# Hourglass attention ahead of a gated FFN on one core: a new order of work in each slot, and small softmax columns moved into PSUM

## The chip, the cores and the metric

The kernel runs on one core of a Trainium2 chip. The metric is device time in microseconds, the median of several executions. The engines named below are the profile's: PE is TensorE (PEld its weight loads), DVE is VectorE, ACT is ScalarE, POOL is GpSimd, SP is SyncE; a "q" behind a name is the engine's instruction queue, which also issues transfers.

## The reference

Two stages in a row. Inputs are q, k and v of shape 8 x 8 x 576 x 64 (batch, heads, tokens, head size) and three FFN matrices, all float32. Cut to what matters:

```
q_d, k_d, v_d = means over 4 tokens in a row            # 576 -> 144 tokens
out_d  = softmax(q_d k_d^T / 8) v_d                     # pooled attention, 144 x 144
local  = softmax over the keys with |i - j| < 4 of (q k^T / 8), times v
x      = repeat(out_d, 4 tokens) + local                # rows (batch, token), 8 heads side by side: 4608 x 512
out    = (relu(x w_gate) * (x w_val)) w_out             # 512 -> 1536 -> 512
```

## The kernel before

**Tiling.** Two heads form a pair, so there are 32 pairs; four pairs fill the 512 columns of one batch of 576 rows of x. For a pair, q and k are loaded as float32 (`nat`), cast to float16 (`h16`, `cast_qk`: the half i=0 on ACT at L222, i=1 on POOL at L224), and turned so that the head size lies on partitions (`qkT`). v is loaded in windows of 32 tokens with a margin of 3 on both sides (`vst`) and cast on POOL (L230). Pairs below `NPE` = 12 are turned by PE matmuls against an identity (`turn_qk_pe`, `t_ps`), from which ACT (L265, two pieces) and DVE (L262, one) copy out of PSUM; pairs from 12 on are turned by DMA transposes that SP issues.

**Attention of a pair.** POOL adds four neighbours of `qkT` in two steps (`pool_qk`: `t`, L275, then `qkd`, L278). PE makes the local scores (36 matmuls into two banks, L288, `s_ps`), the pooled scores (4 matmuls into two banks, L302, `d_ps`), and the pooled v (12 matmuls, L312 and L321, `v_ps`, which ACT copies at L360 to `vd`). The local softmax on DVE adds the mask (L333), takes the row maximum `mx` (L352) and subtracts it (L353); ACT takes the exponential `e` (L381); DVE sums (L386), inverts (`rl`, L388) and multiplies (L393) to the weights `en`. The pooled softmax takes maxima on DVE (`max_d`: L341 twice, scaled to `nb` at L344), exponentials with a running sum on ACT (`exp_d`, L369, two instructions for each of the two heads), the reciprocal `rd` of the sums on DVE (L403) and a multiplication on POOL (`weights_d`, L410: two instructions) to `adn`. Both weights are turned (`turn_a_pe`: PE transposes into `a_ps`, L433 and L438, ACT copies L434 `at` and L439 `adt`; from pair 12 on by DMA). `outputs` then makes the local output (36 matmuls, L448, `u_ps`) and the pooled one (8 matmuls, L465, `o_ps`, which ACT copies to `od`), and DVE adds both into `xT` (L478).

**FFN.** A chunk has 512 rows. A task "h" is 8 matmuls of 512 columns for 128 of the 1536 hidden units (L494, two banks `h1_ps`, `h2_ps`), a Relu on ACT (L502) and a product on DVE (L504); a task "y" is 12 matmuls of 512 columns (L510), an ACT copy (L518) and a store of 128 rows. The list `ffn` holds, for each chunk, four times three h and a y of the chunk before; the first chunk has an empty entry in place of y.

**Order.** The kernel is recorded in a manual order: each engine runs its instructions in the order in which `slot(n)` issues them, and waits only through semaphores. `slot(n)` runs for n from -2 to 33. It handles pair n's scores and softmax, pair n-1's turned weights and outputs (pair n-2's from 12 on), pair n+1's turned q and k and its pooling, and pair n+2's casts (n+3's from 12 on). `quota` lets it take FFN entries: none for n below 4, three for n = 4 to 13, then four. `ffn_do` takes one entry, or none as long as its rows of x aren't made. What remains of the list after the slots runs alone. All PSUM results take turns in one pool of eight banks.

Of the kernel before, what the change touches and what calls it, by code (L numbers as in the profile page):

```python
# [17 lines left out]
VR = 112  # L18


def _np_constants():


    mask = np.full((96, 6, 38), NEG, np.float32)
    for blk in range(6):
        for p in range(96):
            w = 6 * (blk // 2) + 2 * (p // 32) + blk % 2
            t = 32 * w + p % 32
            for c in range(38):
                key = 32 * w - 3 + c  # L30
                if 0 <= key < 576 and abs(key - t) < 4:
                    mask[p, blk, c] = 0.0


    pool = np.zeros((VR, 9, 128), np.float16)
    for l in range(9):
        for par in range(2):
            for r in range(32):
                t = 16 * l + 8 * par + r // 4
                for col in [t] if l < 8 else [t - 128, 96 + t - 128]:  # L40
                    pool[64 * par + 3 + r, l, col] = 0.25
    return mask, pool, np.eye(96, dtype=np.float16)


# [5 lines left out]
def kernel(  # L50
# [57 lines left out]

    cons = pool("consts", 1)
    mask_sb = cons.tile([96, 6, 38], FP32, name="mask_sb")  # L110
    pool_sb = cons.tile([VR, 9, 128], FP16, name="pool_sb")
    eye_sb = cons.tile([96, 96], FP16, name="eye_sb")
    nc.scalar.dma_start(eye_sb, eye_dr)
    nc.scalar.dma_start(mask_sb, mask_dr)
    nc.scalar.dma_start(pool_sb, pool_dr)
    p_v16 = pool("v16", 7)
# [5 lines left out]
    p_ed = pool("ed", 2)  # L122
    p_vd = pool("vd", 4)
    p_od = pool("od", 2)
    psum = ctx.enter_context(tc.tile_pool(name="psum", bufs=8, space=bass.MemoryType.PSUM))

    for t in v_t:
        nc.gpsimd.memset(t[32:64], 0.0)
# [7 lines left out]
    def bank(shape, name, dt=FP32):  # L136
        return psum.tile(shape, dt, name=name, tag="bank")
# [68 lines left out]

    def cast_qk(p, i):
        s = st[p]
        if i == 0:
            s["h16"] = p_16.tile([96, 2, 768], FP16, name="h16", tag="h16")  # L210
        if p < NPE:
            src = s["nat"].rearrange("p a c -> p (a c)").rearrange(
                "p (b h f d) -> p h b f d", b=3, h=2, f=4
            )[:, i]
            dst = s["h16"].rearrange("p a c -> p (a c)").rearrange(
                "p (b f h d) -> p h b f d", b=3, h=2, f=4
            )[:, i]
        else:
            src = s["nat"][:, i].rearrange("p (h j d) -> p h j d", h=2, j=6)
            dst = s["h16"][:, i].rearrange("p (j h d) -> p h j d", h=2, j=6)  # L220
        if i == 0:
            nc.scalar.copy(out=dst, in_=src)  # L222
        else:
            nc.gpsimd.tensor_copy(out=dst, in_=src)  # L224
            s.pop("nat")

    def cast_v(p):
        s = st[p]
# [66 lines left out]

    def scores_d(p):
        s = st[p]
        qkd, v16 = s.pop("qkd"), s["v16"]
        s["dp"] = dp = [bank([80, 2, S // 4], "d_ps") for _ in range(2)]
        for c in range(2):  # L300
            for h in range(2):
                nc.tensor.matmul(  # L302
                    out=dp[h][:, c, :],
                    lhsT=qkd[64 * h : 64 * h + 64, 0, 64 * c : 64 * c + 80],
                    rhs=qkd[64 * h : 64 * h + 64, 1, :],
                    start=True,
                    stop=True,
                )
        s["vp"] = vp = bank([128, 4, D], "v_ps")
        v2 = v16.rearrange("p (h l) d -> p h l d", h=2)  # L310
        for l in range(8):
            nc.tensor.matmul(  # L312
                out=vp[:, 0:2, :],
                lhsT=pool_sb[:, l, :],
                rhs=v2[:, :, l, :],
                start=(l == 0),
                stop=(l == 7),
            )
        for c in range(2):
            for h in range(2):  # L320
                nc.tensor.matmul(  # L321
                    out=vp[64 * h : 64 * h + 64, 2 + c, :],
                    lhsT=pool_sb[:, 8, 64 * c : 64 * c + 64],
                    rhs=v2[:, h, 8, :],
                    start=True,
                    stop=True,
                )
# [9 lines left out]
    def max_d(p):  # L337
        s = st[p]
        s["nb"] = nb = p_st.tile([80, 4], FP32, name="nb", tag="nb")
        for h in range(2):  # L340
            nc.vector.tensor_reduce(  # L341
                out=nb[:, 2 * h : 2 * h + 2], in_=s["dp"][h], axis=AX.X, op=ALU.max
            )
        nc.vector.tensor_scalar(  # L344
            out=nb, in0=nb, scalar1=-SCALE / 16.0, scalar2=None, op0=ALU.mult
        )

    def shift_l(p):

        sm = st[p]["sm"]  # L350
        mx = p_st.tile([96, 12], FP32, name="mx", tag="mx")
        nc.vector.tensor_reduce(out=mx, in_=sm, axis=AX.X, op=ALU.max)  # L352
        nc.vector.tensor_tensor(  # L353
            out=sm, in0=sm, in1=mx[:, :, None].to_broadcast([96, 12, 38]), op=ALU.subtract
        )
# [27 lines left out]
    def sums(p):  # L383
        s = st[p]
        sl = p_st.tile([96, 12], FP32, name="sl", tag="sl")
        nc.vector.tensor_reduce(out=sl, in_=s["e"], axis=AX.X, op=ALU.add)  # L386
        s["rl"] = p_st.tile([96, 12], FP32, name="rl", tag="rl")
        nc.vector.reciprocal(out=s["rl"], in_=sl)  # L388

    def weights_l(p):  # L390
# [33 lines left out]
            out=adt_tile(p), in_=s.pop("ad").rearrange("p a c -> p (a c)")  # L424
        )

    def turn_a_pe(p):
        s = st[p]
        en = s.pop("en").rearrange("p (a b) c -> p a (b c)", b=2)
        s["at"] = p_at.tile([128, 8, 96], FP16, name="at", tag="at")[:, 0:6, :]  # L430
        tp = bank([128, 6, 96], "a_ps", FP16)
        for i in range(6):
            nc.tensor.transpose(tp[:, i, :], en[:, i, :], eye_sb)  # L433
        nc.scalar.copy(out=s["at"], in_=tp)  # L434
        ad = s.pop("ad")
        tp = bank([128, 5, 80], "a_ps", FP16)
        for i in range(5):
            nc.tensor.transpose(tp[:, i, :], ad[:, i, :], eye_sb[0:80, 0:80])  # L438
        nc.scalar.copy(out=adt_tile(p), in_=tp)  # L439

    def outputs(p):
# [15 lines left out]
                        stop=True,  # L457
                    )
        op = bank([128, S // 4], "o_ps")
        for c in range(2):  # L460
            lo, n, skip = (0, 80, 0) if c == 0 else (80, 64, 16)
            for tail in range(2):
                for h in range(2):
                    rows = slice(64 * h, 64 * h + 64) if tail else slice(0, 128)
                    nc.tensor.matmul(  # L465
                        out=op[64 * h : 64 * h + 64, lo : lo + n],
                        lhsT=vd[rows, 2 + c if tail else h, :],
                        rhs=adt[rows, 4 if tail else 2 * h + c, skip : skip + n],
                        start=(tail == 0),
                        stop=(tail == 1),  # L470
                    )
        od = p_od.tile([128, S // 4], FP32, name="od", tag="od")
        nc.scalar.copy(out=od, in_=op)  # L473
# [47 lines left out]
    def store_y():  # L521
        while ysb:
            row, y_sb = ysb.pop(0)
            nc.sync.dma_start(_dap(out, row * DM, [[DM, 128], [1, DM]]), y_sb)
# [25 lines left out]
    def at_stage(p, *fs, pe=None):  # L550
        if 0 <= p < NP and (pe is None or pe == (p < NPE)):
            for f in fs:
                f(p)
# [7 lines left out]
    def slot(n):  # L561
        quota = 0 if n < 4 else 3 if n < 14 else 4
        at_stage(n - 1, turn_a, pe=False)
        at_stage(n + 2, turn_qk, pe=False)
        while loaded[0] < min(NP, n + (5 if n < NPE - 2 else 6)):
            load(loaded[0])
            loaded[0] += 1
        if n == 0:
            at_stage(n, scores, scores_d)
            at_stage(n + 1, turn_qk_pe)  # L570
        else:
            at_stage(n + 1, turn_qk_pe, pe=True)
            at_stage(n, scores, scores_d)
        at_stage(n + 1, pool_qk)
        if 1 <= n < 5:
            load_h_weights(n - 1)
        elif 5 <= n < 9:
            load_y_weights(n - 5)
        at_stage(n + 2, lambda p: cast_qk(p, 0), lambda p: cast_qk(p, 1), cast_v, pe=True)
        at_stage(n, mask_l, max_d, shift_l, copy_vd, lambda p: exp_d(p, 0))  # L580
        store_y()
        if quota > 1:
            ffn_do()
        at_stage(n - 1, turn_a_pe, out_stage, pe=True)
        at_stage(n - 2, out_stage, pe=False)
        at_stage(n, exp_l, lambda p: exp_d(p, 1), sums, weights_l)
        if quota:
            ffn_do()
        at_stage(n, weights_d)
        at_stage(n + 3, lambda p: cast_qk(p, 0), lambda p: cast_qk(p, 1), cast_v, pe=False)  # L590
        if quota > 2:
            ffn_do()
        if quota > 3:
            ffn_do()
# [37 lines left out]
```

## Time and profile before

| what | value |
|---|---|
| median of 3 runs | 433.13 us (432.29 to 435.07) |
| profiled execution, own time | 433.71 us |
| its span in the profile | 431.9 us |
| PE busy | 392.4 us (91%) |
| DVE, ACT, POOL busy | 252.1 us (58%), 211.6 us (49%), 172.8 us (40%) |
| mean granted clock of PE | 0.983 |
| chain that ended last: PE, DVE, ACT | 80%, 9%, 6% of the span |

A profile line for a group of instructions gives the kernel's line, the engine, the operation, output and inputs with their sizes, the count, the busy time, the mean duration in ns, and the idle time of the engine just ahead of them with what ended most of it. A timeline line gives start and length in us, then the same; in square brackets stands how long the engine was idle ahead of it and whose instruction it had waited for. A run of equal instructions is drawn as one line, so its length is that of the run. Times count from the start of the span.

### The profile page before, as it was taken

How to read it: one execution, taken by the hardware profiler on the slowest of the kernel's cores; microseconds unless marked ns; L12 is line 12 of the kernel's file. 1: busy time of each engine (PE TensorE's matmuls, PEld its weight loads, DVE VectorE, ACT ScalarE, POOL GpSimd, SP SyncE). 2: the span in 40 equal slices, each digit the busy share in tenths (PEclk: the TensorE clock that was granted, in tenths of full speed). 3: DMA queues.
4: the chain of work that ended last, by engine and by line, in shares of the span. 5: the costliest groups of instructions: out<-in, count | busy, mean ns of one | idle time of the engine just before them, and what ended most of it. 6: DMA issues, size and time to landing. Idle time of an engine off the chain costs nothing.

```text
span 431.9 us, 11627 instructions
## 1 busy us (share of the span) xinstructions
PE 392.4 (91%) x4644; PEld 205.7 (48%) x4644; DVE 252.1 (58%) x542; ACT 211.6 (49%) x577; POOL 172.8 (40%) x219
## 2 busy tenths in 40 slices
PE   0475798889899999999999999999999999999996
PEld 0364554446455555555555545555554444444442
DVE  1476687788677976666666666666665322222210
ACT  1566666557455655555555555555444323233221
POOL 4888755555445744444444444454311000000000
PEclk9999998889899999999999999999999999999999
DMA  8999999970795898999989999975411001010012
GB/s 180 228 222 233 227 224 220 162 129 15 174 198 125 173 186 182 171 173 185 175 174 191 183 183 188 189 147 90 89 49 49 25 26 49 24 50 24 26 49 97
DMA packets 167259, 59.19 MB, mean 137 GB/s; under 512 B 149846, under 2 KB 162486, under 8 KB 167206
## 3 DMA queue, kind: packets, MB, share of 16 engines
q1 hardware_dynamic: 161030, 53.38, 61.3%
q0 software_dynamic: 5824, 4.72, 7.3%
q8 instruction: 36, 0.59, 0.6%
q10 hardware_dynamic: 352, 0.36, 0.4%
q14 instruction: 17, 0.14, 0.1%
HBM read 42.83 MB, written 9.44 MB: 121 GB/s over the span
## 4 chain that ended last, share of the span: by engine, by line
PE 80%; DVE 9%; ACT 6%; issue 2%; DMA 1%; POOL 0%; SPq 0%; ACTq 0%; DVEq 0%; POOLq 0%
PE h_ps L494 43%; PE y_ps L510 22%; PE o_ps L465 5%; PE u_ps L448 3%; PE v_ps L312 3%; ACT ed L369 2%; DVE nb L341 2%; PE s_ps L288 2%; DVE sm L333 2%; ACT at L434 1%; DVE nb L344 1%; DMA nat<-in_k_dram 1%; PE d_ps L302 1%; DVE qkT L262 1%; PE v_ps L321 1%
## 5 line engine op out<-in xcount | busy, mean ns | idle before, releaser
L504 DVE TENSOR_TENSOR g<-r,h_ps 128x512 f16<-128x512 f16 x108 | 74.0, 685 | 124.1 <-PE h_ps L494 118.3
L494 PE MATMUL h_ps<-xT,wg_sb 128*128 128x512 f16 x432 | 115.5, 391 | 0.0
L494 PE MATMUL h_ps<-xT,wv_sb 128*128 128x512 f16 x432 | 114.9, 390 | 0.0
L410 POOL TENSOR_TENSOR adn<-ed,rd 80x512 f16<-80x512 f16 x64 | 41.2, 663 | 144.7 <-ACT h L222 74.2
L510 PE MATMUL y_ps<-wo_sb,g 128*128 128x512 f16 x432 | 98.7, 380 | 0.0
L502 ACT ACTIVATE r<-h_ps 128x512 f16<-128x512 f32 x108 | 64.0, 592 | 39.4 <-PE h_ps L494 39.3
L494 PEld LDWEIGHTS <-wv_sb 128*128 128x128 f16 x432 | 43.3, 100 | 54.2 <-issue 5.6
L510 PEld LDWEIGHTS <-g 128*128 128x128 f16 x432 | 42.3, 98 | 51.2 <-issue 0.8
L369 ACT ACTIVATE ed<-d_ps,nb 80x144 f16<-80x144 f32 x128 | 46.8, 369 | 29.6 <-DVE nb L344 29.6
L494 PEld LDWEIGHTS <-wg_sb 128*128 128x128 f16 x432 | 38.6, 99 | 42.6 <-issue 3.8
L518 ACT COPY y_sb<-y_ps 128x512 f32<-128x512 f32 x36 | 21.1, 586 | 76.1 <-PE y_ps L510 76.0
L275 POOL TENSOR_TENSOR t<-qkT 128x576 f32<-128x576 f16 x32 | 36.6, 1144 | 3.8 <-DVE qkT L262 2.6
L230 POOL CAST v<-vst 112x1152 f16<-112x1152 f32 x32 | 36.8, 1150 | 2.3 <-DMA vst<-in_v_dram 2.3
L478 DVE TENSOR_TENSOR xT<-u_ps,od 128x288 f16<-128x288 f32 x64 | 26.2, 451 | 17.7 <-ACT od L473 16.7
L448 PE MATMUL u_ps<-at,v 38*64 38x32 f16 x1152 | 15.6, 185 | 18.7 <-ACT at L434 18.7
L353 DVE TENSOR_TENSOR sm<-sm,mx 96x456 f32<-96x456 f32 x32 | 28.4, 889 | 1.1
L360 ACT CAST vd<-v_ps 128x256 f16<-128x256 f32 x32 | 11.9, 373 | 34.3 <-PE v_ps L321 33.9
L224 POOL CAST h<-nat 96x768 f16<-96x768 f32 x32 | 26.8, 839 | 3.5 <-DMA nat<-in_k_dram 3.5
L222 ACT CAST h<-nat 96x768 f16<-96x768 f32 x32 | 26.7, 834 | 1.0 <-DMA nat<-in_k_dram 1.0
L448 PEld LDWEIGHTS <-v 38*64 38x64 f16 x1152 | 13.8, 114 | 27.6 <-issue 26.3
L341 DVE TENSOR_REDUCE nb<-d_ps 80x2 f32<-80x288 f32 x64 | 25.9, 444 | 0.0
L369 ACT ACTIVATION_READ_ACCUMULATOR ed<-d_ps,nb 80x1 f32 x128 | 24.7, 193 | 0.0
(45 smaller groups left out, 371.4 us busy)
## 6 DMA issues: line engine op xcount, KB each, us to landing
vst<-in_v_dram SPq DMA_DIRECT2D x62, 216.0 KB, 4.7
out_dram<-y_sb SPq DMA_DIRECT2D x36, 256.0 KB, 2.3
nat<-in_q_dram SPq DMA_DIRECT2D x20, 288.0 KB, 3.5
nat<-in_k_dram SPq DMA_DIRECT2D x20, 288.0 KB, 4.3
nat<-in_q_dram SPq DMA_DIRECT2D x12, 192.0 KB, 6.9
nat<-in_k_dram SPq DMA_DIRECT2D x12, 192.0 KB, 5.6
wg_sb<-in_moe_w_gate_dram POOLq DMA_DIRECT2D x4, 384.0 KB, 7.0
wv_sb<-in_moe_w_val_dram POOLq DMA_DIRECT2D x4, 384.0 KB, 9.2
```

The lines of the kernel that those rows point to most:

```text
L224: nc.gpsimd.tensor_copy(out=dst, in_=src)
L230: nc.gpsimd.tensor_copy(out=s["v16"], in_=s.pop("vst"))
L275: nc.gpsimd.tensor_tensor(out=t1, in0=qkv[:, :, :, 0], in1=qkv[:, :, :, 1], op=ALU.add)
L341: nc.vector.tensor_reduce(out=nb[:, 2 * h : 2 * h + 2], in_=s["dp"][h], axis=AX.X, op=ALU.max)
L353: nc.vector.tensor_tensor(out=sm, in0=sm, in1=mx[:, :, None].to_broadcast([96, 12, 38]), op=ALU.subtract)
L369: nc.scalar.activation(out=s["ed"][:, i, :], in_=s["dp"][h][:, c, :], func=AF.Exp, scale=SCALE / 16.0, bias=s["nb"][:, i : i + 1], accum_o ...
L410: nc.gpsimd.tensor_tensor(out=o, in0=i, in1=rd[:, :, None].to_broadcast([80, 4, n]), op=ALU.mult)
L448: nc.tensor.matmul(out=up[par][64 * h : 64 * h + 64, l, :], lhsT=v16[64 * par : 64 * par + 38, 9 * h + l, :], rhs=at[64 * par : 64 * par + 38,
L494: nc.tensor.matmul(out=h, lhsT=w[:, kk, bass.ts(jj, 128)], rhs=xT[:, kk, bass.ts(c, TCH)], start=(kk == 0), stop=(kk == 3),)
L502: nc.scalar.activation(out=r, in_=h1, func=AF.Relu)
L504: nc.vector.tensor_tensor(out=g, in0=r, in1=h2, op=ALU.mult)
L510: nc.tensor.matmul(out=y, lhsT=gts[c][jj][:, bass.ts(ty, 128)], rhs=wo_sb[:, jj, :], start=(jj == 0), stop=(jj == NJJ - 1),)
```

## The change

The edits, one by one:

- In `slot`, PE's order becomes: scores of n (local, then pooled), turned local weights of n-1, pooled v of n, turned pooled weights of n-1, the first FFN entry, turned q and k of n+1, outputs of n-1, further FFN entries. `turn_a_pe` is cut in two for this (`turn_en_pe`, `turn_ad_pe`), `scores_d` too (`pool_v` holds the pooled v).
- On DVE the local softmax up to the subtraction stands ahead of the pooled maxima; the copy of `qkT` follows them. On ACT the copy of the turned local weights comes first, the local exponential ahead of the pooled ones, and the cast of n+2 near the end of the slot.
- On POOL the casts of n+2 stand ahead of the weights of n, and `pool_qk(n+1)` behind these (for pairs from 12 on it stands ahead of them). The weight loads of the FFN, which POOL issues, follow.
- The pooled scores have a pool of two PSUM banks for themselves; six are left for all else. `mx`, `rl` and the raw pooled maxima `nbr` are no longer tiles in SBUF but spare columns of those two banks: `mx` beside the scores of the first head, `rl` and `nbr` beside those of the second.
- The matrix that pools v becomes one band of 256 columns of which each matmul takes a window (28,672 float16 values in place of 129,024). A first Exp on a two-column tile stands ahead of everything on ACT. The eight `o_ps` matmuls run in another order, their stores of y are issued at another place of the slot.

```diff
@@ consts
-    pool_sb = cons.tile([VR, 9, 128], FP16, name="pool_sb")
+    pool_sb = cons.tile([VR, 256], FP16, name="pool_sb")
+    warm = cons.tile([128, 2], FP32, name="warm")
+    nc.vector.memset(warm, 0.0)
     nc.scalar.dma_start(eye_sb, eye_dr)
+    nc.scalar.activation(out=warm, in_=warm, func=AF.Exp)
...
-    psum = ctx.enter_context(tc.tile_pool(name="psum", bufs=8, space=bass.MemoryType.PSUM))
+    psum = ctx.enter_context(tc.tile_pool(name="psum", bufs=6, space=bass.MemoryType.PSUM))
+    psum_d = ctx.enter_context(tc.tile_pool(name="psum_d", bufs=2, space=bass.MemoryType.PSUM))
@@ def scores_d(p):
-        s["dp"] = dp = [bank([80, 2, S // 4], "d_ps") for _ in range(2)]
+        db = [psum_d.tile([96, 320], FP32, name="d_ps", tag="d") for _ in range(2)]
+        s["dp"] = dp = [t[0:80, 0:288].rearrange("p (c t) -> p c t", c=2) for t in db]
+        s["mx"], s["rl"], s["nbr"] = db[0][:, 288:300], db[1][:, 288:300], db[1][0:80, 304:308]
...
+    def pool_v(p):
...
@@ def max_d(p):
+        nbr = s.pop("nbr")
         for h in range(2):
             nc.vector.tensor_reduce(
-                out=nb[:, 2 * h : 2 * h + 2], in_=s["dp"][h], axis=AX.X, op=ALU.max
+                out=nbr[:, 2 * h : 2 * h + 2], in_=s["dp"][h], axis=AX.X, op=ALU.max
             )
         nc.vector.tensor_scalar(
-            out=nb, in0=nb, scalar1=-SCALE / 16.0, scalar2=None, op0=ALU.mult
+            out=nb, in0=nbr, scalar1=-SCALE / 16.0, scalar2=None, op0=ALU.mult
         )
@@ def shift_l(p):
-        mx = p_st.tile([96, 12], FP32, name="mx", tag="mx")
+        mx = s.pop("mx")
@@ def sums(p):
-        s["rl"] = p_st.tile([96, 12], FP32, name="rl", tag="rl")
         nc.vector.reciprocal(out=s["rl"], in_=sl)
@@ def slot(n):
-        if n == 0:
-            at_stage(n, scores, scores_d)
-            at_stage(n + 1, turn_qk_pe)
-        else:
-            at_stage(n + 1, turn_qk_pe, pe=True)
-            at_stage(n, scores, scores_d)
-        at_stage(n + 1, pool_qk)
+        store_y()
+        at_stage(n, scores, scores_d)
+        at_stage(n - 1, turn_en_pe, pe=True)
+        at_stage(n, pool_v, mask_l, shift_l, copy_vd, exp_l, max_d)
+        at_stage(n - 1, turn_ad_pe, pe=True)
+        at_stage(n + 2, cast_qk_pool, pe=True)
+        if n > 1:
+            at_stage(n + 2, cast_v, pe=True)
+        at_stage(n + 1, pool_qk, pe=False)
+        if quota > 1:
+            ffn_do()
+        at_stage(n, lambda p: exp_d(p, 0))
+        at_stage(n + 1, turn_qk_pe, pe=True)
+        at_stage(n - 1, out_stage, pe=True)
+        at_stage(n - 2, out_stage, pe=False)
+        at_stage(n, sums, weights_l, lambda p: exp_d(p, 1))
+        at_stage(n + 2, cast_qk_act, pe=True)
+        if quota:
+            ffn_do()
+        at_stage(n, weights_d)
+        at_stage(n + 1, pool_qk, pe=True)
+        if n <= 1:
+            at_stage(n + 2, cast_v, pe=True)
+        at_stage(n + 3, cast_qk_act, cast_qk_pool, cast_v, pe=False)
         if 1 <= n < 5:
             load_h_weights(n - 1)
         elif 5 <= n < 9:
             load_y_weights(n - 5)
-        at_stage(n + 2, lambda p: cast_qk(p, 0), lambda p: cast_qk(p, 1), cast_v, pe=True)
-        at_stage(n, mask_l, max_d, shift_l, copy_vd, lambda p: exp_d(p, 0))
-        store_y()
-        if quota > 1:
-            ffn_do()
-        at_stage(n - 1, turn_a_pe, out_stage, pe=True)
-        at_stage(n - 2, out_stage, pe=False)
-        at_stage(n, exp_l, lambda p: exp_d(p, 1), sums, weights_l)
-        if quota:
-            ffn_do()
-        at_stage(n, weights_d)
-        at_stage(n + 3, lambda p: cast_qk(p, 0), lambda p: cast_qk(p, 1), cast_v, pe=False)
```

More of the change, by code (lines that the diff above doesn't have):

```diff
@@ L32, in _np_constants @@
                     mask[p, blk, c] = 0.0
[L35 to L41, printed above, removed]
+    pool = np.zeros((VR, 256), np.float16)
+    for par in range(2):
+        for r in range(32):
+            pool[64 * par + 3 + r, 128 + 8 * par + r // 4] = 0.25
     return mask, pool, np.eye(96, dtype=np.float16)
@@ L208, in cast_qk @@
         s = st[p]
-        if i == 0:
+        if "h16" not in s:
             s["h16"] = p_16.tile([96, 2, 768], FP16, name="h16", tag="h16")
@@ L224, in cast_qk, with cast_qk_act, cast_qk_pool @@
             nc.gpsimd.tensor_copy(out=dst, in_=src)
-            s.pop("nat")
+    def cast_qk_act(p):
+        cast_qk(p, 0)
+    def cast_qk_pool(p):
+        cast_qk(p, 1)
     def cast_v(p):
@@ L297, in scores_d @@
         s = st[p]
-        qkd, v16 = s.pop("qkd"), s["v16"]
-        s["dp"] = dp = [bank([80, 2, S // 4], "d_ps") for _ in range(2)]
+        qkd = s.pop("qkd")
+        db = [psum_d.tile([96, 320], FP32, name="d_ps", tag="d") for _ in range(2)]
+        s["dp"] = dp = [t[0:80, 0:288].rearrange("p (c t) -> p c t", c=2) for t in db]
+        s["mx"], s["rl"], s["nbr"] = db[0][:, 288:300], db[1][:, 288:300], db[1][0:80, 304:308]
         for c in range(2):
@@ L308, in scores_d @@
                 )
+    def pool_v(p):
+        s = st[p]
+        v16 = s["v16"]
         s["vp"] = vp = bank([128, 4, D], "v_ps")
@@ L313, in scores_d @@
                 out=vp[:, 0:2, :],
-                lhsT=pool_sb[:, l, :],
+                lhsT=pool_sb[:, 128 - 16 * l : 256 - 16 * l],
                 rhs=v2[:, :, l, :],
@@ L322, in scores_d @@
                     out=vp[64 * h : 64 * h + 64, 2 + c, :],
-                    lhsT=pool_sb[:, 8, 64 * c : 64 * c + 64],
+                    lhsT=pool_sb[:, 128 - 32 * c : 192 - 32 * c],
                     rhs=v2[:, h, 8, :],
@@ L339, in max_d @@
         s["nb"] = nb = p_st.tile([80, 4], FP32, name="nb", tag="nb")
+        nbr = s.pop("nbr")
         for h in range(2):
             nc.vector.tensor_reduce(
-                out=nb[:, 2 * h : 2 * h + 2], in_=s["dp"][h], axis=AX.X, op=ALU.max
+                out=nbr[:, 2 * h : 2 * h + 2], in_=s["dp"][h], axis=AX.X, op=ALU.max
             )
         nc.vector.tensor_scalar(
-            out=nb, in0=nb, scalar1=-SCALE / 16.0, scalar2=None, op0=ALU.mult
+            out=nb, in0=nbr, scalar1=-SCALE / 16.0, scalar2=None, op0=ALU.mult
         )
     def shift_l(p):
-        sm = st[p]["sm"]
-        mx = p_st.tile([96, 12], FP32, name="mx", tag="mx")
+        s = st[p]
+        sm = s["sm"]
+        mx = s.pop("mx")
         nc.vector.tensor_reduce(out=mx, in_=sm, axis=AX.X, op=ALU.max)
@@ L425, in turn_a, with turn_en_pe @@
         )
-    def turn_a_pe(p):
+    def turn_en_pe(p):
         s = st[p]
@@ L434, in turn_a_pe, with turn_ad_pe @@
         nc.scalar.copy(out=s["at"], in_=tp)
-        ad = s.pop("ad")
+    def turn_ad_pe(p):
+        ad = st[p].pop("ad")
         tp = bank([128, 5, 80], "a_ps", FP16)
@@ L459, in outputs @@
         op = bank([128, S // 4], "o_ps")
-        for c in range(2):
-            lo, n, skip = (0, 80, 0) if c == 0 else (80, 64, 16)
-            for tail in range(2):
+        for tail in range(2):
+            for c in range(2):
+                lo, n, skip = (0, 80, 0) if c == 0 else (80, 64, 16)
                 for h in range(2):
@@ L468, in outputs @@
                         rhs=adt[rows, 4 if tail else 2 * h + c, skip : skip + n],
-                        start=(tail == 0),
-                        stop=(tail == 1),
+                        start=(tail == 0 and c == 0),
+                        stop=(tail == 1 and c == 1),
                     )
```

## The prediction, made before the changed kernel ran

> **What bounds the kernel now.** I read the 40 slices first. PE is the busiest engine, but it fills its slices only from the thirteenth on, about 140 us:
>
> ```profile
> PE   0475798889899999999999999999999999999996
> PEclk9999998889899999999999999999999999999999
> ```
>
> Next the chain that ended last, in order of time. From 139 us the pooled output (L465) returns every 10.32 us with PE work alone in between. There PE is the bound, its order is nearly that of before, and a change on another engine gives nothing. All that can be gained or lost lies in slots 0 to 12, up to the pooled scores of pair 12 at 128.63 us. So I read PE's timeline there; slot 3, without FFN work, looks like this:
>
> ```profile
> 35.80 1.14 PE L253 MATMUL t_ps<-eye_sb,h 96*128 96x96 f16 x12
> 36.87 0.47 PE L288 MATMUL s_ps<-qkT 64*32 64x38 f16 x36
> 37.28 0.46 PE L302 MATMUL d_ps<-qkd 64*80 64x144 f16 x4
> 37.67 1.03 PE L312 MATMUL v_ps<-v,pool_sb 112*128 112x128 f16 x8
> 38.63 0.32 PE L321 MATMUL v_ps<-v,pool_sb 112*64 112x64 f16 x4
> 38.88 0.66 PE L433 MATMUL a_ps<-eye_sb,en 96*128 96x96 f16 x6
> 39.66 0.51 PE L438 MATMUL a_ps<-eye_sb,adn 80*128 80x80 f16 x5
> 42.51 0.67 PE L448 MATMUL u_ps<-at,v 38*64 38x32 f16 x36 [2.33 <-ACT at L434]
> 43.10 0.87 PE L465 MATMUL o_ps<-adt,vd 128*64 128x80 f16 x8
> ```
>
> PE idles 2.33 us ahead of `u_ps`: ACT copies `at` behind the pooled exponentials, and these wait for the maxima. The period from `d_ps` to `d_ps` is 8.28 us (37.28 to 45.56). No line waits for `qkd`. POOL's timeline says why: in slot 3 it makes `qkd` for the next slot, after the weights of the slot before:
>
> ```profile
> 38.57 1.29 POOL L410 TENSOR_TENSOR adn<-ed,rd 80x512 f16<-80x512 f16 x2 [1.74 <-DVE rd L403]
> 39.82 1.14 POOL L275 TENSOR_TENSOR t<-qkT 128x576 f32<-128x576 f16 x1
> 41.04 0.67 POOL L278 TENSOR_TENSOR qkd<-t 128x288 f16<-128x288 f32 x1
> ```
>
> **What the change takes away.** (1) The wait at `u_ps`: 1.46 us in slot 1, 2.33 in each of slots 2 to 4, then 0.68, 2.09, 1.35, 1.90, 0.65, 1.80, 0.95 and 0.78; 18.7 us in all. `at` becomes ACT's first work of the slot. (2) A slow stretch of PE behind the longer waits:
>
> ```profile
> 71.18 0.46 PE L448 MATMUL u_ps<-at,v 38*64 38x32 f16 x36 [2.09 <-ACT at L434]
> 71.58 0.68 PE L465 MATMUL o_ps<-adt,vd 128*64 128x80 f16 x8
> 72.18 1.88 PE L494 MATMUL h_ps<-xT,wg_sb 128*128 128x512 f16 x4
> 73.86 1.91 PE L494 MATMUL h_ps<-xT,wv_sb 128*128 128x512 f16 x4
> ...
> 77.56 1.04 PE L494 MATMUL h_ps<-xT,wg_sb 128*128 128x512 f16 x4
> ```
>
> Four matmuls take 1.9 us in place of 1.04 for about 3.4 us, then run at full speed again. This follows the waits of 1.35 us and more, not those of 0.95 and less: 1.7 us per task h, five times. (3) DVE's subtraction (L353) lasts 3.12 us at 90.92 us while POOL is busy from 89.00 to 93.55, and 0.63 at the median. It reads two SBUF tiles; with `mx` in PSUM it reads one. I cost it at 0.63, and the maxima, the reciprocal and the products at their present rows. Nearest rows for a PSUM operand: L504, 0.69 us for 512 columns against 0.63 for 456; 0 to 0.06 each, I take 0.
>
> **What it adds: a closed loop.** `pool_qk(n+1)` now stands on POOL behind the weights of n, and `d_ps` of n+1 stands early in PE's slot n+1. Behind `d_ps` PE holds everything else of the slot, so the outputs of n; DVE adds these ahead of its sums of n+1; and those lead to the weights that POOL needs before the next `qkd`. One turn of this loop is one slot. In a slot without FFN, from the start of `d_ps`, at the starts of slot 3's lines:
>
> - PE: `d_ps` 0.39, turned `en` 0.48, pooled v 1.21, turned `adn` 0.45, turned q and k 1.07, `u_ps` 0.60, `o_ps` 0.87: end at 5.07.
> - ACT's `od` 0.04 later; DVE's L478 0.32 after its start, and from there 0.74, 0.65, 0.26 and 0.63 to the end of `en`: 7.71.
>
> ```profile
> 36.06 0.82 DVE L478 TENSOR_TENSOR xT<-u_ps,od 128x288 f16<-128x288 f32 x2 [2.15 <-ACT od L473]
> 36.80 0.61 DVE L386 TENSOR_REDUCE sl<-e 96x12 f32<-96x456 f16 x1
> 37.44 0.23 DVE L388 RECIPROCAL rl<-sl 96x12 f32<-96x12 f32 x1
> 37.70 0.63 DVE L393 TENSOR_TENSOR en<-e,rl 96x456 f16<-96x456 f16 x1
> 38.25 0.17 DVE L403 RECIPROCAL rd<-sd 80x4 f32<-80x4 f32 x1
> ```
>
> - The second half of the pooled exponentials reads the bank that `rl` lies in, and in the built program it waits for the multiplication that reads `rl`: hop 0.1, two instructions with their accumulator reads 0.83 (41.10 to 41.93), `rd` at 8.7.
> - POOL: `adn` 0.32 after `rd` starts, `t` 1.25 later, `qkd` 1.22 later, and `d_ps` 0.72 after that (13.24 to 13.96): **12.2 us**, against 8.28.
>
> DVE's `mx` writes into the bank of `d_ps`, so the local softmax also waits for `d_ps`; but it is done by 2.7 us, inside PE's 5.07.
>
> In a slot with FFN at full PE speed the steps are 0.26, 0.27, 0.73, 0.29, the first entry 1.74, 0.61, 0.40, 0.67: `o_ps` ends at 4.97, `en` at 7.6, the exponentials start at 7.7. Three kinds of slot follow. If the second entry is an h, ACT casts n+2 first (0.73), then does its Relu (0.60, 9.16 to 9.76), DVE's product starts at 9.8 and `rd` stands behind it (0.61): 10.4, and with POOL's 3.5 the turn is **13.9** (slots 6 and 7). If it is empty, `rd` starts at 8.6: **12.1** (slots 5 and 9). If the first entry is empty instead, `od` waits for ACT until 4.2, and the turn is **13.15** (slot 8). Slot 10 casts nothing ahead of the Relu: 13.2. Slot 4, with slow matmuls and no first entry: 7.8 + 0.73 + 0.6 + 0.14 + 0.61 + 0.35 + 3.2 = 14.0 with rounding.
>
> PE has 7.3 to 9.1 us of work in such a slot, so it idles about 5. Behind an idle time so long it should be slow at the start of every slot. I take the 3.4 us stretch of the rows and half a microsecond, 3.9 in all: the four small steps at the no-FFN rows (2.53 for 1.55) and 1.15 us of h done in twice the time: 1.55 us per slot, slots 5 to 10. Bounds: 0, and 3.5 where the whole path runs slow (1.7 more for h, 1.9 more for the rest).
>
> **The other edits.** The ACT table load (1.28 us at 8.03) goes behind the first loads. But `pool_qk(0)` now stands behind the cast of pair 1, whose k lands at 12.7 (ACT's cast waits for it until 12.78): cast 0.82, `t` 1.22, `qkd` 0.72, first `d_ps` at 15.5 in place of 13.96. Slot 0 has no outputs: `en` at 4.7, `rd` 5.75, `d_ps` of pair 1 after 9.3. Six banks in place of eight: each `t_ps`, `u_ps` or `h_ps` takes the bank of the sixth result before it, read out long before in the loop above; up to 0.3 us a slot where not, I take 0. The smaller constant and the moved weight and y transfers meet slots that are longer than now, so their buffers wait less; 0, at most 1 us either way. The order of the `o_ps` matmuls keeps eight of them (0.6 to 0.9). POOL's casts ahead of its weights take 2 us (0.77 and 1.16) and lie in the 8.7 us or more in which POOL waits for `rd`: 0; without that cover they would add 2 us a slot, which a late load alone could bring, and loads get more time, not less.
>
> **The sum.** `d_ps` of pair 11: 15.5 + 9.3 + 3 x 12.2 + 14.0 + (12.1 + 13.9 + 13.9 + 13.15 + 12.1 + 13.2) + 6 x 1.55 = 163.0 us; it is at 119.43 now. From slot 11 on `pool_qk` stands ahead again and the loop is open; the waits of 0.95 and 0.78 go, a last slow start costs 1.55: -0.2. So the profiled execution of 433.71 us (span 431.9, 1.8 outside) becomes 433.7 + 43.6 - 0.2 = 477.1. The median of the runs is 0.6 lower: **476.5**.
>
> **Two rules of the Trainium skill.** "SBUF — State Buffer", section "Who interferes with whom", says that a DVE instruction with two SBUF inputs contends with POOL's reads; the 3.12 us row agrees. By this rule alone the change gains the surplus of L353, 28.4 - 32 x 0.63 = 8.2 us of DVE time at most. "PSUM — Partial Sum Buffer", section "PSUM bank collisions raise a hardware error", speaks against it: two engines mustn't be in one bank and quadrant at once, even at other addresses, so columns beside the scores tie ACT to DVE. Without that tie `rd` could follow `en` at 7.65, and the sum would be lower by about 1 us in slots without an h as second entry and 2 in those with one, some 15 us.
>
> **Rivals.** *The loop, with PE at full speed* (0.20): PE's idle time doesn't slow it; 476.5 - 7 x 1.55 = 466. Full speed behind the waits of 0.65 to 0.95 us speaks for it; against it, the idle times to come are longer than all that slowed PE. *The loop, with PE slow throughout slots 5 to 10* (0.13): 6 x 1.95 more, 488. *The loop doesn't close, faster* (0.05): if `qkd` reaches PE within the 9.1 us of work that PE has ahead of it, the waits (18.7) and slow stretches (8.5) go and 406 is left; POOL's 3.5 us behind `rd` would need `rd` at 5.6, ahead of DVE's own L393, so the rows speak against it. *It cancels out* (0.03): that needs turns of about 10.3 us, as PE's work and the present slots have. Some part in between (0.07): 440 to 458. My forecast has 0.52.
>
> **Range and chances.** 457 to 489 takes in the forecast and both other forms of the loop: 0.85. One per cent is about what a measurement of this kernel can tell from no change. Slower by more: 0.92; within: 0.03; faster: 0.05.
>
> **What the changed profile would show.** Right: the first weights of `d_ps` wait 3 to 5 us for POOL `qkd` in slots 1 to 10; `d_ps` to `d_ps` is 12 us in slots 1 to 3 and 12 to 16 in 5 to 10; the idle time of `u_ps` on `at` is gone; L353 stays near 0.63; from slot 13 the 10.32 us period returns. Wrong: if `d_ps` waits for little, or if POOL's `adn` starts earlier than 8 us into a slot.

## The result, and where it shows in the profile

| | before | changed |
|---|---|---|
| median | 433.65 us (432.29 to 435.07, 4 runs) | 475.5 us (474.33 to 477.72, 4 runs) |
| profiled execution, its span | 433.71 us, 431.9 us | 474.33 us, 472.6 us |
| PE busy, mean granted clock | 91%, 0.983 | 84%, 0.955 |

The ratio is 1.0971, with a 95% interval of 1.0916 to 1.1026: 9.7% slower. The forecast was 476.5 us, in a range of 457 to 489.

The 40 slices of the changed kernel (each 11.8 us; PE busy and granted clock in tenths):

```profile
PE   1244495755669799999999999989999999999996
PEclk9999999759777799999999999999999999999999
```

The second half still looks as before. Nearly all of the loss lies in the first fifteen slices, and with it a granted clock that drops to 0.5 to 0.7 in six of them, where the kernel before shows 0.8 in four. PE's timeline of slot 3, from one `d_ps` to the next (start and busy time in us, engine, line and operation; in brackets the wait ahead of it in us, and what ended it):

```profile
47.15 0.46 PE L311 MATMUL d_ps<-qkd 64*80 64x144 f16 x4 [6.49 <-POOL qkd L284]
47.55 0.66 PE L447 MATMUL a_ps<-eye_sb,en 96*128 96x96 f16 x6
48.01 1.05 PE L325 MATMUL v_ps<-v,pool_sb 112*128 112x128 f16 x8
48.99 0.32 PE L334 MATMUL v_ps<-v,pool_sb 112*64 112x64 f16 x4
49.24 0.51 PE L454 MATMUL a_ps<-eye_sb,adn 80*128 80x80 f16 x5
49.55 1.16 PE L259 MATMUL t_ps<-eye_sb,h 96*128 96x96 f16 x12
50.65 0.67 PE L464 MATMUL u_ps<-at,v 38*64 38x32 f16 x36
51.24 0.59 PE L481 MATMUL o_ps<-adt,vd 128*64 128x80 f16 x8
51.76 0.68 PE L294 MATMUL s_ps<-qkT 64*32 64x38 f16 x36
58.94 0.46 PE L311 MATMUL d_ps<-qkd 64*80 64x144 f16 x4 [6.49 <-POOL qkd L284]
```

The wait at `u_ps` for `at` is gone, as intended. In its place stands 6.49 us ahead of `d_ps`, on POOL. The first twelve `d_ps` wait so, 59.3 us in all. The turn is 11.79 us; the slot of before took 8.28. What POOL waits for in slot 2, first in DVE's timeline:

```profile
42.13 0.62 DVE L407 TENSOR_TENSOR en<-e,d_ps 96x456 f16<-96x456 f16 x1
43.64 0.17 DVE L417 RECIPROCAL rd<-sd 80x4 f32<-80x4 f32 x1 [0.89 <-ACT ed L384]
```

then in ACT's:

```profile
42.78 0.38 ACT L384 ACTIVATE ed<-d_ps,nb 80x144 f16<-80x144 f32 x1 [2.34 <-DVE en L407]
```

and POOL's own:

```profile
43.97 1.28 POOL L424 TENSOR_TENSOR adn<-ed,rd 80x512 f16<-80x512 f16 x2 [4.05 <-DVE rd L417]
45.22 1.13 POOL L281 TENSOR_TENSOR t<-qkT 128x576 f32<-128x576 f16 x1
46.44 0.66 POOL L284 TENSOR_TENSOR qkd<-t 128x288 f16<-128x288 f32 x1
```

This is the chain of the prediction, line by line: ACT's second pooled exponentials wait 2.34 us for DVE's `en`, `rd` waits for ACT, `adn` for `rd`, and `t` and `qkd` stand behind `adn`.

| step | predicted us | measured us |
|---|---|---|
| first `d_ps` | 15.5 | 14.53 |
| turn of slot 0 | 9.3 | 9.11 |
| slots 1 to 3 | 12.2 each | 11.72, 11.79, 11.79 |
| slot 4 | 14.0 | 13.62 |
| slots 5, 6, 7 | 13.65, 15.45, 15.45 | 11.65, 15.45, 16.23 |
| slots 8, 9, 10 | 14.7, 13.65, 14.75 | 13.61, 13.13, 14.52 |
| `d_ps` of pair 11 (before: 119.43) | 163.0 | 157.15 |
| shift from there to the end | -0.2 | +3.0 |

The last row is the span's shift of 40.7 us less the 37.7 us at pair 11. The total was closer (476.5 for the median of 475.5; 477.1 for the profiled 474.33) than its parts: 5.9 us too much up to pair 11, 3.2 too little behind it. That much of its closeness is luck, since the two errors have opposite signs. The experiments name both.

### The profile page after: what moved, and what is told of

Read it like the earlier page. It is cut to its first block, busy times and chain, and to the rows that moved or that the text cites. A ratio compares the mean times of both kernels' runs of the same rounds, so it can differ in the third digit from the quotient of the medians.

```text
span 472.6 us, 11651 instructions
## 1 busy us (share of the span) xinstructions
PE 394.8 (84%) x4644; PEld 204.4 (43%) x4644; DVE 247.2 (52%) x543; ACT 208.9 (44%) x578; POOL 170.9 (36%) x219
## 4 chain that ended last, share of the span: by engine, by line
PE 65%; POOL 8%; DVE 8%; ACT 8%; DMA 4%; issue 4%; SPq 1%; POOLq 0%; ACTq 0%; DVEq 0%
PE h_ps L510 33%; PE y_ps L526 19%; PE v_ps L325 3%; POOL adn L424 3%; ACT ed L384 3%; POOL t L281 3%; DMA nat<-in_k_dram 3%; PE u_ps L464 2%; PE o_ps L481 2%; PE d_ps L311 2%; ACT r L518 2%; DVE xT L494 2%; POOL qkd L284 2%; DVE en L407 1%; DMA vst<-in_v_dram 1%
## 5 line engine op out<-in xcount | busy, mean ns | idle before, releaser
L510 PE MATMUL h_ps<-xT,wg_sb 128*128 128x512 f16 x432 | 117.8, 397 | 0.0
L510 PEld LDWEIGHTS <-wv_sb 128*128 128x128 f16 x432 | 43.0, 100 | 58.6 <-issue 12.2
L311 PE MATMUL d_ps<-qkd 64*80 64x144 f16 x128 | 12.0, 268 | 59.9 <-POOL qkd L284 59.3
L367 DVE TENSOR_REDUCE d_ps<-sm 96x12 f32<-96x456 f32 x32 | 20.2, 631 | 34.9 <-PE d_ps L311 32.9
L396 ACT ACTIVATE e<-sm 96x456 f16<-96x456 f32 x32 | 18.6, 582 | 41.3 <-DVE sm L368 41.3
L311 PEld LDWEIGHTS <-qkd 64*80 64x80 f16 x128 | 5.6, 124 | 62.0 <-POOL qkd L284 60.7
L355 DVE TENSOR_REDUCE d_ps<-d_ps 80x2 f32<-80x288 f32 x64 | 29.3, 458 | 1.1
L448 ACT COPY at<-a_ps 128x576 f16<-128x576 f16 x12 | 7.7, 638 | 44.6 <-PE a_ps L447 44.6
```

Source lines behind the costliest of these rows:

```text
L311: nc.tensor.matmul(out=dp[h][:, c, :], lhsT=qkd[64 * h : 64 * h + 64, 0, 64 * c : 64 * c + 80], rhs=qkd[64 * h : 64 * h + 64, 1, :], start ...
L355: nc.vector.tensor_reduce(out=nbr[:, 2 * h : 2 * h + 2], in_=s["dp"][h], axis=AX.X, op=ALU.max)
L510: nc.tensor.matmul(out=h, lhsT=w[:, kk, bass.ts(jj, 128)], rhs=xT[:, kk, bass.ts(c, TCH)], start=(kk == 0), stop=(kk == 3),)
```

## Experiments

The theory: the slowdown is one closed loop, POOL's `pool_qk` behind `weights_d`; the columns in the bank of the pooled scores lengthen it; PE's slow starts come from its idle time. Rivals: six banks in place of eight, or the reordering as such. The runs were made on several chips, on which the kernel before measured 431.8 to 433.7 us, so a difference between two versions that were run on different chips is good to about 2 us.

### One line moved in the changed kernel: pooling early

```diff
         at_stage(n + 1, turn_qk_pe, pe=True)
+        at_stage(n + 1, pool_qk, pe=True)
...
         at_stage(n, weights_d)
-        at_stage(n + 1, pool_qk, pe=True)
```

> The changed kernel with one line moved: pooling of pair n+1 (pairs below 12) is issued right behind the turning of its q and k, so on POOL it stands ahead of the weights of n. Loop theory: the pooled scores no longer wait for POOL qkd; the next loop runs through the turned pooled weights (weights, turned adn, first FFN entry, turned q and k, outputs, sums, weights): by the rows about 8.3 us in slots without FFN and 10.5 to 11 us with an h as second entry, so 430 to 442 us. Rival 'six banks or the bank tie slow it': the pooled scores' wait goes but the time stays above 460.

Measured: 436.9 us, 1.012 times before (1.007 to 1.017). One line takes back 38.6 of the 42 us. Two of PE's waits, both in slot 7, now read:

```profile
74.65 0.28 PE L311 MATMUL d_ps<-qkd 64*80 64x144 f16 x3 [1.07 <-ACT ed L384]
77.89 0.52 PE L454 MATMUL a_ps<-eye_sb,adn 80*128 80x80 f16 x5 [1.96 <-POOL adn L424]
```

From pair 5 on no `d_ps` waits for `qkd`; the first five still do, 12.0 us in all. The next loop, through `adn`, holds PE as foreseen, and the second bank of `d_ps` waits for the exponentials of the pair before.

### The inverse sums back in SBUF

```diff
 def sums(p):
+        s["rl"] = p_st.tile([96, 12], FP32, name="rl", tag="rl")
         nc.vector.reciprocal(out=s["rl"], in_=sl)
```

> The changed kernel with the inverse sums rl back in their own SBUF tile, so the second half of the pooled exponentials has no column of DVE's in its bank to wait for. The loop stays. By the rows the reciprocal of the pooled sums starts about 1 us earlier in slots without an h as second entry and 2 us in those with one: some 15 us less, 458 to 464 us. Rival 'the tie costs nothing, DVE's own order sets the reciprocal': within 1% of 475.5 us.

Measured: 451.1 us, 1.044 times before (1.039 to 1.049), 24.4 less than the changed kernel and so more than either theory said. The turn of slot 3 is 10.81 us (44.51 to 55.32) in place of 11.79, the foreseen 1 us:

```profile
44.51 0.46 PE L311 MATMUL d_ps<-qkd 64*80 64x144 f16 x4 [5.51 <-POOL qkd L284]
55.32 0.46 PE L311 MATMUL d_ps<-qkd 64*80 64x144 f16 x4 [5.51 <-POOL qkd L284]
```

Up to pair 11 the gain is 13.1 us (157.15 to 144.07), about what was expected. The rest lies where I had looked for nothing. Pair 14's `d_ps` comes at 168.30 us in place of 185.66, and the span ends 23.2 us earlier. From pair 14 on the changed kernel has a period of 10.22 us with two longer slots, this one 10.09 without one. The tie also holds up PE where PE is the bound. Its waits there, from the changed kernel's list of who waited for whom from 150 us on (us in total, times, longest); the list also has pair 11's last wait for `qkd`, 3.3 us, and three of 0.2 to 0.5:

```profile
PE h_ps L510 <- ACT r L518: 1.9, 2, 1.0
PE u_ps L464 <- DVE sm L346: 0.7, 1, 0.7
PE d_ps L311 <- ACT ed L384: 0.6, 1, 0.6
```

ACT, which waits 72.0 us in all at the exponentials for DVE's `en`, reads PE's banks out late. With `rl` in SBUF the same list is empty.

### Both edits

The diff is the sum of the two above.

> Both edits of the two runs before on the changed kernel: pooling early and rl in SBUF. Loop theory: the remaining loop is 7.4 us without FFN and about 8.7 us with, below PE's 9.1 us of work per FFN slot, so PE's waits and its slow stretches mostly go: 408 to 420 us, faster than the kernel before. Rival 'the gains don't add up, since PE stays slow or POOL and DVE block each other at the product with rl': 428 to 440 us.

Measured: 415.2 us, 0.961 times before (0.957 to 0.965). With the loop open and the tie gone, the reordering does what it set out to do. PE in slot 6, which the first line opens:

```profile
62.73 0.32 PE L311 MATMUL d_ps<-qkd 64*80 64x144 f16 x4
63.22 0.43 PE L448 MATMUL a_ps<-eye_sb,en 96*128 96x96 f16 x6 [0.17 <-DVE en L408]
...
64.49 0.46 PE L455 MATMUL a_ps<-eye_sb,adn 80*128 80x80 f16 x5 [0.21 <-POOL adn L425]
...
68.09 0.44 PE L482 MATMUL o_ps<-adt,vd 128*64 128x80 f16 x8 [0.26 <-DVE g L521]
```

From there on what is left of PE's waits is 0.2 to 1.1 us each; the first five `d_ps` still wait for `qkd`, 12.6 us in all. The granted clock is 0.994. DVE's product with `rl`, now with two SBUF inputs, takes 0.63 us at the median and 1.0 at most, so this column did not need PSUM.

### One line moved in the kernel before: pooling late

```diff
-        at_stage(n + 1, pool_qk)
+        at_stage(n + 1, pool_qk, pe=False if n >= 0 else None)
...
         at_stage(n, weights_d)
+        if n >= 0:
+            at_stage(n + 1, pool_qk, pe=True)
```

> The kernel before with one line moved: pooling of pair n+1 (pairs below 12, from slot 0 on) stands on POOL behind the weights of n, as in the changed kernel; all else as before. Loop theory: 12.8 us per slot without FFN in place of 8.3 and 12 to 13.5 with FFN in place of about 10.3, so 460 to 470 us; the pooled scores wait 3 to 5 us for POOL qkd. Rival 'the other reordering makes the slowness': within 2% of 433 us.

Measured: 463.2 us, 1.074 times before (1.068 to 1.079). The same move alone, in the old order and with eight banks, makes most of the slowdown:

```profile
36.37 0.46 PE L302 MATMUL d_ps<-qkd 64*80 64x144 f16 x4 [4.52 <-POOL qkd L278]
47.70 0.46 PE L302 MATMUL d_ps<-qkd 64*80 64x144 f16 x4 [4.58 <-POOL qkd L278]
```

The turn is 11.33 us, not the expected 12.8: once PE stands still ahead of `d_ps`, `at` and the outputs no longer wait as long as they did in the rows I added up (PE's wait for `at` in slot 3 is 1.22 us, for 2.33 before).

### Two banks apart, in the kernel before

```diff
-    psum = ctx.enter_context(tc.tile_pool(name="psum", bufs=8, space=bass.MemoryType.PSUM))
+    psum = ctx.enter_context(tc.tile_pool(name="psum", bufs=6, space=bass.MemoryType.PSUM))
+    psum_d = ctx.enter_context(tc.tile_pool(name="psum_d", bufs=2, space=bass.MemoryType.PSUM))
...
-        s["dp"] = dp = [bank([80, 2, S // 4], "d_ps") for _ in range(2)]
+        s["dp"] = dp = [psum_d.tile([80, 2, S // 4], FP32, name="d_ps", tag="d") for _ in range(2)]
```

> The kernel before with the pooled scores in a pool of two PSUM banks and six for all else; nothing else changed. Theory: the sixth result before is always read out in time, so within 0.5% of before. Rival 'six banks hold PE up': PE waits for bank readers appear from 140 us on and the time is over 438 us.

Measured: 433.2 us, 1.001 times before (0.999 to 1.004). Six banks cost nothing that this measurement can tell in the old order.

### Extra matmuls in PE's idle time

```diff
-        at_stage(n, scores, scores_d)
+        at_stage(n, scores)
+        keep_busy({5: 18, 6: 36, 7: 50, 8: 38, 9: 28, 10: 36, 11: 24}.get(n, 0))
+        at_stage(n, scores_d)
...
+    def keep_busy(k):
+        if k:
+            x = bank([128, 256], "x_ps")
+            for _ in range(k):
+                nc.tensor.matmul(out=x, lhsT=pool_sb[:, 0:128], rhs=pool_sb, start=True, stop=True)
```

> The changed kernel with extra matmuls of 256 columns, whose result nobody reads, between the local and the pooled scores of slots 5 to 11: 18, 36, 50, 38, 28, 36 and 24 of them, about 0.108 us each at full speed, which fills most of PE's idle time there. Theory 'idle time slows PE in the first microseconds of the next slot, inside the loop': the slow stretches of slots 6 to 11 go, 2.0, 2.7, 1.8, 1.5, 1.8 and about 2 us, so 462 to 467 us. Rival 'PE's pace there has nothing to do with idle time, or lies beside the loop': 473 to 480 us.

Measured: 463.1 us, 1.072 times before (1.067 to 1.076): 12.4 us less than the changed kernel, with 230 matmuls of useless work more; the granted clock rises from 0.955 to 0.999. Slot 7, first in the changed kernel, then with the extra work:

```profile
99.66 0.46 PE L311 MATMUL d_ps<-qkd 64*80 64x144 f16 x4 [6.67 <-POOL qkd L284]
...
102.06 1.91 PE L510 MATMUL h_ps<-xT,wg_sb 128*128 128x512 f16 x4
103.76 1.91 PE L510 MATMUL h_ps<-xT,wv_sb 128*128 128x512 f16 x4
```

```profile
89.99 5.63 PE L575 MATMUL x_ps<-pool_sb 112*128 112x256 f16 x50
96.75 0.32 PE L311 MATMUL d_ps<-qkd 64*80 64x144 f16 x4 [1.12 <-POOL qkd L284]
...
98.18 1.03 PE L510 MATMUL h_ps<-xT,wg_sb 128*128 128x512 f16 x4
99.05 1.03 PE L510 MATMUL h_ps<-xT,wv_sb 128*128 128x512 f16 x4
```

Four matmuls take 1.03 us in place of 1.91, and the turn of slot 7 falls from 16.23 to 13.61 us (96.75 to 110.36). The prediction's turns at full speed were all close: 12.1, 13.9, 13.9, 13.15, 12.1 and 13.2 us for slots 5 to 10, against 11.65, 13.50, 13.61, 13.11, 11.65 and 12.76 here. The slow start is shown to come from the idle time. Not all of the 12.4 us is the extra work's: in the two profiles slots 5 to 10 get 8.3 us shorter and slot 11 2.9, while the first `d_ps` merely came 1.0 earlier.

How long PE must idle is not shown. The prediction saw slow starts behind waits of 1.35 us and more and none behind 0.95 and less, but the changed kernel's slot 5 starts at full speed behind 2.73 us:

```profile
72.56 0.32 PE L311 MATMUL d_ps<-qkd 64*80 64x144 f16 x4 [2.73 <-POOL qkd L284]
...
74.00 1.03 PE L510 MATMUL h_ps<-xT,wg_sb 128*128 128x512 f16 x4
```

and in the kernel with both edits PE is slow behind 1.05:

```profile
84.10 0.45 PE L482 MATMUL o_ps<-adt,vd 128*64 128x80 f16 x8 [1.05 <-ACT adt L456]
84.66 1.87 PE L511 MATMUL h_ps<-xT,wg_sb 128*128 128x512 f16 x4
```

So the length of the last wait alone does not decide it.

### All small columns back in SBUF

On top of the kernel with both edits:

```diff
-        s["mx"], s["rl"], s["nbr"] = db[0][:, 288:300], db[1][:, 288:300], db[1][0:80, 304:308]
...
-        nbr = s.pop("nbr")
+        nbr = p_st.tile([80, 4], FP32, name="nbr", tag="nbr")
...
-        mx = s.pop("mx")
+        mx = p_st.tile([96, 12], FP32, name="mx", tag="mx")
```

> The kernel with pooling early and rl in SBUF, now with the row maxima mx and the raw pooled maxima in SBUF too, so that no small column is in PSUM. Theory 'small columns in PSUM keep DVE clear of POOL': the subtraction and the scaling of the maxima are held up by POOL again in some slots, up to 3 us each, 2 to 8 us more than 415.2 us. Rival 'the hold-ups lie off the path, and the local softmax gains by not waiting for the pooled scores': 411 to 416 us.

Measured: 430.0 us, 0.994 times before (0.992 to 0.997), so 14.9 us more than with `mx` and `nbr` in PSUM. The sign was right, the size twice what I allowed. DVE in slot 7 of this kernel:

```profile
79.81 3.35 DVE L367 TENSOR_TENSOR sm<-sm,mx 96x456 f32<-96x456 f32 x1
```

and PE behind it:

```profile
84.21 0.20 PE L464 MATMUL u_ps<-at,v 38*64 38x32 f16 x2 [1.70 <-ACT adt L455]
```

The subtraction, 0.62 us with `mx` in PSUM in every slot, takes 3.35 here while POOL multiplies, issues a load and casts from 78.71 to 82.68. "SBUF — State Buffer", section "Who interferes with whom", in the Trainium skill says that DVE with two SBUF inputs contends with POOL's reads; these rows agree. The subtraction ended only 0.48 us after the last of these POOL instructions. Over the 32 pairs DVE's subtraction takes 40.9 us in place of 20.0, its scaling of the maxima 8.6 in place of 5.0, so most of the hold-up is at `mx`, though the two were not tried apart. In the new order ACT's local exponential waits for the subtraction, and the copy of `adt` stands behind it, so the hold-up reaches PE: its waits for `adt` at `u_ps` and `o_ps` come to 8.7 us, against 1.0 with `mx` and `nbr` in PSUM. In the old order ACT waited for the subtraction 1.7 us in all.

### The order of the pooled output's matmuls

In the changed kernel the eight `o_ps` matmuls take less time than before. This order alone, in the kernel before:

```diff
-        for c in range(2):
-            lo, n, skip = (0, 80, 0) if c == 0 else (80, 64, 16)
-            for tail in range(2):
+        for tail in range(2):
+            for c in range(2):
+                lo, n, skip = (0, 80, 0) if c == 0 else (80, 64, 16)
...
-                        start=(tail == 0),
-                        stop=(tail == 1),
+                        start=(tail == 0 and c == 0),
+                        stop=(tail == 1 and c == 1),
```

> The kernel before with the eight o_ps matmuls in the new order alone (four with 128 rows, then four with 64). In the changed kernel they take 0.37 us up to the next matmul, in the kernel before 0.61, and the period from 140 us on is 10.09 in place of 10.32 us where nothing else holds PE. Theory 'each switch between full and half rows costs PE time': 0.24 us in each of 32 slots, 7.7 us less where PE is the bound, so 424 to 427 us. Rival 'the shorter o_ps comes from the other reordering around it': within 0.5% of before.

Measured: 425.5 us, 0.983 times before (0.979 to 0.986). In the first fence, of the kernel before, the next matmul starts 0.61 us after `o_ps`; in the second, with the new order alone, 0.37:

```profile
149.22 0.68 PE L465 MATMUL o_ps<-adt,vd 128*64 128x80 f16 x8
149.83 1.04 PE L494 MATMUL h_ps<-xT,wg_sb 128*128 128x512 f16 x4
```

```profile
155.63 0.44 PE L465 MATMUL o_ps<-adt,vd 128*64 128x80 f16 x8
156.00 1.04 PE L494 MATMUL h_ps<-xT,wg_sb 128*128 128x512 f16 x4
```

Two edits are in that diff, so the marks were tried alone: the old order, with

```diff
-                        start=(tail == 0),
-                        stop=(tail == 1),
+                        start=(tail == 0 and c == 0),
+                        stop=(tail == 1 and c == 1),
```

> The kernel before with the o_ps matmuls in their old order, and only the marks of the first and last matmul of a sum as in the changed kernel (one first and one last per head in place of two). Theory 'the order is what costs': 433 us, within 0.5% of before. Rival 'the marks cost': 425 us.

Measured: 433.0 us, 1.001 times before (0.999 to 1.003). The order is what counts. The third order, in the kernel before and in the one with both edits:

```diff
-        for tail in range(2):
+        for tail in (1, 0):
...
-                        start=(tail == 0 and c == 0),
-                        stop=(tail == 1 and c == 1),
+                        start=(tail == 1 and c == 0),
+                        stop=(tail == 0 and c == 1),
```

> The kernel before with the eight o_ps matmuls in a third order: the four with 64 rows first, right behind the u_ps matmuls, which use at most 64 rows too, then the four with 128 rows ahead of the FFN's. Theory 'each change between 64 and 128 rows costs PE 0.12 us': two changes fewer per slot than in the changed kernel's order and four fewer than before, 0.48 us in 32 slots, 15 us: 417 to 420 us. Rival 'it is not the change of rows': 425 us as in the changed kernel's order, or 433.

Measured: 420.9 us, 0.974 times before (0.970 to 0.977), just above the expectation: the late period falls from 10.33 to 9.99 us, by 0.34 and not by 0.48.

> The kernel with pooling early and rl in SBUF (415.2 us), with the four o_ps matmuls of 64 rows ahead of those of 128. Theory of the row changes: 0.24 us less in 32 slots, 7.7 us, so 406 to 409 us. Rival: 413 to 416 us.

Measured: 412.7 us, 0.955 times before (0.951 to 0.959), the lowest median here; but 2.5 us below the one with both edits, where 7.7 was expected. The intervals of the two just overlap, but the period falls from 10.09 to 9.99 us, by 0.10 and not by 0.24. "TensorEngine Tiling (Array Packing)", section "Key Properties", in the Trainium skill says that a change of tiling mode drains the engine; the order of 64 and 128 rows does cost time here, but, counted by rows, not a fixed 0.12 us per change: two changes less inside `o_ps` saved 0.24, two less at its ends 0.10. Counting rows alone may be the mistake. In the profile's forms the FFN's matmuls hold 128*128 weights and the `o_ps` ones of 128 rows only 128*64, so a change remains between them in the third order; counted by rows and columns, it has one change less for its 0.10 us. No run separates the two counts, so what sets the cost of one change stays open.

## Why the prediction was right, and where its parts were off

- **The loop** (predicted turns of 12.2 us without FFN and 12.1 to 13.9 with it, before slow starts) is shown from both sides: taking it out of the changed kernel gives back 38.6 us, putting it alone into the kernel before costs 31.4 (463.2 against the 431.8 of the same chip). The waits ahead of `d_ps` were 2.73 to 6.67 us in slots 1 to 10, 6.4 to 6.5 in slots 2 to 4, not the "3 to 5" named as a sign; the prediction's own turn of 12.2, less PE's 5.07 and 0.6 for the local scores, gives 6.5. Its terms for slot 4 add up to 13.4, not 14.0; measured 13.62.
- **The tie through the bank** was priced rightly inside the loop (1 us in slot 3; 13.1 us up to pair 11 for an expected 15 in all). The step that failed is "from slot 11 on the loop is open: -0.2". The tie delays ACT in every slot, so PE waits for banks even where it is the bound: with `rl` in SBUF the part from pair 14 to the end takes 5.8 us less. Together with a slower slot 11 (10.83 us for 9.20 before) it turned -0.2 into +3.0.
- **The slow starts**, 1.55 us in each of slots 5 to 10, 9.3 in all. The extra matmuls gave back 8.3 in these six slots, so the sum was near. Singly they were uneven: none in slot 5, where PE had been idle for 2.73 us, 0.5 in slot 8 behind 4.95, 2.6 in slot 7 behind 6.67. (The working takes 1.15 us of h into the slow stretch; its 3.9 less 2.53 leaves 1.37, which is 0.1 us more per slot.)
- **"The order of the `o_ps` matmuls keeps eight of them (0.6 to 0.9)", costed at nothing**: the mis-sized term. It is worth 0.24 us a slot where PE is the bound (7.5 us in the kernel before) and shortens the loop too: `o_ps` takes 0.52 to 0.59 of the 0.87 that the walk gave it. Most of the 0.4 us by which the turns of slots 1 to 3 came out short is here. It is also why the late period is not the 10.32 us that the prediction named as a sign: this order alone gives 10.09 in the kernel before, and the tie adds 0.13 to make 10.22.
- **The first `d_ps`** came at 14.53 for 15.5: pair 1's k landed a microsecond earlier than in the profile before, so POOL cast it from 11.73. Such a shift is no sign of the order: in the runs on the changed kernel the first `d_ps` came between 13.49 and 15.13.
- **Six banks at nothing** was right, as the two-bank run shows for the old order; in the new one PE's list of waits from 150 us on is empty with six banks once `rl` is in SBUF.
- **The columns in PSUM at "8.2 us of DVE time at most"** was about right as DVE time: the subtraction went from 28.4 to 20.0 us, while the pooled maxima, now written to PSUM, went from 25.9 to 29.3. It is no bound on the kernel's time: in the new order, with the loop open, `mx` and `nbr` there are worth 14.9 us, since DVE's subtraction now leads to PE.

So the change holds two bad edits, pooling behind the weights and `rl` in the bank of the pooled scores; without them it takes 415.2 us in place of 475.5. Of the rest, the `o_ps` order is good by itself (425.5 us in the kernel before). The new order of the slot is good only with `mx` and `nbr` in PSUM: the new order with all columns in SBUF takes 430.0 us, 4.6 more than the old order with the new `o_ps` order, on the same chip; with the two columns in PSUM it takes 415.2. The columns in the old order were not run, and the small edits (the band matrix, the first Exp, the place of the casts) were not tried alone.

## What to carry to other kernels

When an order is changed in a software pipeline, follow each queue past a slot's end: an operation that feeds the start of the next slot must not stand behind one that needs the end of this one, or a whole slot's latency becomes the period. A spare column of a PSUM bank kept DVE clear of POOL here, but it makes an engine that still has to read that bank wait until the column is done with; and once PE idles for microseconds, count its slow start as well. An order that puts an operation on the path pays only if that operation is kept short: try such edits together and apart. In a kernel bound by PE, the order of matmuls that use 64 and 128 rows is worth a run, since a trace of one order can't price the other.

## What the runs showed of the hardware that I had not expected

- Eight small matmuls in another order, with the same operands, take 0.37 in place of 0.61 us until the next one starts, and 1.7% of the kernel's time. The marks of first and last have no part in it (433.0 us).
- PE fed with useless matmuls makes the kernel 12.4 us faster, 11.2 of them in the slots that got them (5 to 11): four matmuls of 512 columns go from 1.91 to 1.03 us when the idle time ahead of them shrinks from 6.67 to 1.12 us.
- A DVE subtraction of 0.62 us takes up to 3.35 us beside POOL when its second input lies in SBUF, and 0.62 for all 32 pairs when it lies in PSUM.
